# Strassen's seven half-size products for the first feed-forward matrix too, and a batch laid out as values, gate, keys, gate

## The chip, the cores and the metric

The kernel runs on one core of one Trainium2 chip. The metric is device microseconds of one execution. Engines are named as the profile names them: PE (TensorE matmuls), PEld (its weight loads), DVE (VectorE), ACT (ScalarE), POOL (GpSimd) and SP (SyncE, which here issues every DMA). All data are float32; most matrices of the feed-forward part are held as a rounded high part and a low part (`float32r`), and a product of two such matrices takes three matmuls: high by high, high by low, low by high.

## The reference, cut to what matters

```python
s = scale * q @ k^T        # 8 batches, 8 heads, 512 local and 32 global tokens, head size 64
out_l = softmax(s over 32 global keys and a window of +-32) @ v ;  out_g = softmax(all) @ v
x = both, as (batch 8, 576 tokens, 512)
xk = mu_k * x + (1 - mu_k) * x_prev ;  xr = mu_r * x + (1 - mu_r) * x_prev
k = maximum(xk @ w_k, 0.0)                    # w_k: 512 x 1024, "keys"
v = k * k @ w_v                               # w_v: 1024 x 512, "values"
return 1 / (1 + exp(-(xr @ w_r))) * v         # w_r: 512 x 512, the "gate"
```

Weights arrive as float64 words and are decoded on the chip.

## The kernel before, in words

Features lie on the partitions. A batch of 512 local tokens is two halves of 256 tokens (`TOK`), each a `Tokens` object; the 256 global tokens of all batches are one more, done last. For a half, `mix` (L499) makes the high and low parts of xk and xr (DVE, a rounding copy on ACT at L516, the rest on POOL at L517); `squares` (L540) does the keys: per PSUM bank 24 matmuls of 128x256 (`products`, L483 to L485: two blocks of 128 features, four blocks of the sum, three matmuls), then a relu on ACT (L549) and a multiplication on DVE (L551); `gates` (L554) does two banks of 24 and takes tanh on ACT (L564, L566).

The values are Strassen's already, from batch 2 on (`FROM`). With the left matrix cut in 2x2 blocks A and the right one (features by two token halves) in blocks B, seven products replace eight. Sums of blocks of the weights are made once, during batch 1 (`sums_of_values`, L223), and all eight left matrices are kept in DRAM (`scratch`). `load_left` (L253) brings them back in parts of 512 KB, one DMA each, through the five buffers of `leftp`; a product (L632) is 24 matmuls at L639 and uses two parts. `differences` (L614) and `split` (L622) make the right blocks and their high and low parts (ACT L201, then DVE or POOL L202). Three products stand before the keys of a batch's first half (`values_1`), four before those of the second (`values_2`); so a batch goes values, keys, gate, values, keys, gate. Results are multiplied into the gate's tile (`write`, L582) and stored.

Attention for the next batch runs beside the feed-forward part of this one: `together` (L773) deals out steps of the two streams at build time, and a scheduler that plays a timeline then orders each engine's instructions; on the chip each engine runs its list strictly in order. The steps of attention that matter below are the scores (L350), the exponentials (L324: eight in a row on ACT), the scaling (L334 on POOL), transposes (L371, L380, L421) and the weighted sums (L350 again, 117 matmuls in one go). PSUM has eight banks: three ("m") serve the feed-forward part from batch 2 on, four the scores, one the transposes. The last batch and the global tokens have no attention beside them.

Of the kernel before, what the change touches and what calls it, by code (L numbers as in the profile page):

```python
# [55 lines left out]
def local_global_attention_then_rwkv_ffn(  # L56
# [34 lines left out]
    ps2 = ctx.enter_context(tc.tile_pool(name="ps2", bufs=2, space=PSUM))  # L91
# [6 lines left out]
    FIRST_USE = {"m": [ps2] * 2, "s": [ps4] * 4, "t": [ps1, psx], "o": "t"}  # L98
    MIDDLE_USE = {"m": [ps2, ps2, psx], "s": [ps4] * 4, "t": [ps1], "o": "s"}
    LAST_USE = {"m": [ps2, ps2, psx, ps4, ps4, ps4, ps4]}  # L100
# [45 lines left out]
    wk_h = const.tile([P, NC, DF], F32R, name="wk_h")  # L146
    wk_l = const.tile([P, NC, DF], F32R, name="wk_l")

    early_w, early_u = ExitStack(), ExitStack()
    first_chunks = early_w.enter_context(tc.tile_pool(name="first_chunks", bufs=1, reuse_waits="tile"))
# [13 lines left out]
    def load_chunk():  # L166
        n = load_chunk.n
        if n < len(chunks):
            if n < EARLY:
                w64 = first_chunks.tile([P, CH], I64, tag=f"w64_{n}", name="w64")  # L170
            else:
                w64 = stage.tile([P, CH], I64, tag="w64", name="w64")
            nc.sync.dma_start(out=w64, in_=chunks[n][0])
            staged.append(w64)
            load_chunk.n += 1
# [41 lines left out]

    FROM = 2
    LEFT = ("A11", "A21", "A12", "A22", "S2", "S3", "S4", "S1")
    HC = NF // 2  # L220
    scratch = dramp.tile([P, len(LEFT), HC, 2, TOK], F32, name="scratch")

    def sums_of_values():  # L223
        for i in range(HC):
            a = stage.tile([P, 2, 2, TOK], F32, tag="w64", name="a")
            hs, ls = (stage.tile([P, 4, TOK], F32R, tag="w64", name=f"{x}s") for x in "hl")
            for j in range(2):
                f = i + j * HC
                for x, part in enumerate((wv_h, wv_l)):
                    part = part[:, f].bitcast(F32).rearrange("p (e n) -> p e n", e=2)  # L230
                    nc.sync.dma_start(out=scratch[:, 2 * j:2 * j + 2, i, x], in_=part)
                nc.gpsimd.tensor_add(
                    a[:, j], *(w[:, f].bitcast(F32).rearrange("p (e n) -> p e n", e=2) for w in (wv_h, wv_l))
                )
            a11, a21, a12, a22 = (a[:, j, e] for j in range(2) for e in range(2))

            nc.gpsimd.tensor_add(a22, a21, a22)
            nc.gpsimd.tensor_sub(a21, a11, a21)
            nc.gpsimd.tensor_sub(a11, a22, a11)
            nc.gpsimd.tensor_sub(a12, a12, a11)  # L240
            s = a.rearrange("p j e n -> p (j e) n")
            nc.scalar.copy(hs, s)
            nc.vector.tensor_sub(ls, s, hs.bitcast(F32))
            for x, part in enumerate((hs, ls)):
                nc.sync.dma_start(out=scratch[:, 4:8, i, x], in_=part.bitcast(F32))
            yield

    V1 = (("A11", "B11"), ("A12", "B21"), ("S2", "T2"))
    V2 = (("S3", "T3"), ("S1", "T1"), ("A22", "T4"), ("S4", "B22"))
    to_load = [a for a, _ in V1 + V2] * (B - FROM) + ["A11", "A21", "A12", "A22"]  # L250
    left = []

    def load_left():  # L253
        if to_load:
            a = LEFT.index(to_load.pop(0))
            for i in range(0, HC, 2):
                part = leftp.tile([P, 2, 2, TOK], F32R, tag="a", name="a")
                nc.sync.dma_start(out=part.bitcast(F32), in_=scratch[:, a, i:i + 2])
                left.append(part)
# [227 lines left out]
    class Tokens:  # L487
# [5 lines left out]
        def two(self, pool, name, dtype=F32, tag="tmp"):  # L493
            return pool.tile([P, 2, TOK], dtype, tag=tag, name=name)
# [4 lines left out]
        def mix(self):  # L499

            got = []
            for mu, nm in ((mu_k_sb, "k"), (mu_r_sb, "r")):
                got.append((mu, self.wide(f"x{nm}h", F32R), self.wide(f"x{nm}l", F32R)))
            for c0 in range(0, NC, 2):
# [4 lines left out]
                for mu, hi, lo in got:  # L509
                    xf = self.two(tmpp, "xfull")  # L510
                    for j in range(2):
# [3 lines left out]
                        )  # L515
                    nc.scalar.copy(hi[:, both], xf)  # L516
# [3 lines left out]
        def keys_and_gate(self):  # L520
            self.kk_h, self.kk_l = [], []
            for f0 in range(0, NF, 2):
# [7 lines left out]
                nc.gpsimd.tensor_mul(k2, rk, rk)  # L530
# [23 lines left out]
        def gates(self, pool=None):  # L554

            pool = pool or gatep
            self.gate = pool.tile([P, NC, TOK], F32, tag="gate", name="gate")
            for e0 in range(0, NC, 2):
# [4 lines left out]
                with tc.high_priority(None if pool is not gatep else 0):  # L563
# [24 lines left out]

    class Keys:


        def __init__(self, tokens):
            self.tokens = tokens
            self.k, self.parts = {}, {}

# [5 lines left out]
        def block(self, name):  # L601
            if name in ("B12", "B22"):
                tag = {"B12": "kkh0", "B22": "kkh2"}[name]
                self.k[name] = [self.tokens[0].two(mlp, name, tag=tag) for _ in range(2)]
# [5 lines left out]
        def keys(self, t):  # L610
# [11 lines left out]
        def split(self, *names):  # L622
            for b in names:
                self.parts[b] = []
                for val in self.k[b]:
                    tags = Keys.PARTS[Keys.n_parts % len(Keys.PARTS)]
                    Keys.n_parts += 1
                    h, l = (self.tokens[0].two(mlp, f"b{x}", F32R, tag) for x, tag in zip("hl", tags))
# [3 lines left out]
        def product(self, out, b, fresh=True):  # L632
            right = self.parts.pop(b)
            for i in range(HC):
                a, (b_h, b_l) = left[i // 2], right[i // 2]
                for j in range(2):
                    a_h, a_l = (a[:, i % 2, x, j * P:(j + 1) * P] for x in range(2))
# [382 lines left out]
```

## Time and profile before

| | |
|---|---|
| three timed executions | 700.31, 703.33, 703.79 us; median 703.33 us |
| the profiled execution | 702.47 us, of which the span of instructions is 700.6 us |
| mean granted TensorE clock | 0.978 |
| DMA | 123.37 MB, mean 176 GB/s over the span |

Rows of the profile: a group of instructions gives line, engine, operation, what it writes and reads, shape and count, then its busy time in us and the mean length of one in ns, then the idle time of the engine just ahead of it and what ended it. A matmul's length runs from its start to its modelled end; several overlap. Windows give each engine's busy time and number of instructions in a stretch, the granted clock, and the share and rate of the DMA engines. In a timeline the first two numbers are start and length in us.

### The profile page before, as it was taken

What the parts mean: (1) busy time and instruction counts of PE and PEld (TensorE: products, weight loads), DVE (VectorE), ACT (ScalarE), POOL (GpSimd) and SP (SyncE); (2) the same over time, 40 slices, a digit from 0 to 9 for tenths busy, and PEclk for the clock granted to TensorE, in tenths of its full rate; (3) what the DMA queues carried; (4) which work ended last, traced back from release to release, by engine and by line L of the source; (5) the groups of instructions that cost most, each with busy time, mean ns of one, the idle gap of its engine ahead of it and who ended that gap; (6) DMA issues with size and microseconds to landing.
All of it is one profiled execution on the core that took longest, in us unless ns stands there. A gap on an engine that the chain in (4) does not pass through costs nothing.

```text
span 700.6 us, 18622 instructions
## 1 busy us (share of the span) xinstructions
PE 667.4 (95%) x7472; PEld 629.2 (90%) x7472; DVE 417.7 (60%) x1217; ACT 387.9 (55%) x1058; POOL 357.2 (51%) x363
## 2 busy tenths in 40 slices
PE   4879989988999999999999999999999999999997
PEld 2658778978999999999999999999999999999996
DVE  5767977635635375645684557645674656477531
ACT  5756876447445456656557473757465643442530
POOL 5656597864524334573428353645348332642800
PEclk9659999999999999999999999999999999999999
DMA  8732579462312452362909083635727090534665
GB/s 344 288 99 109 200 215 338 157 237 80 127 71 92 132 216 76 122 242 75 359 20 338 25 312 140 222 140 175 279 89 274 2 352 11 196 121 166 216 189 198
DMA packets 43542, 123.37 MB, mean 176 GB/s; under 512 B 4032, under 2 KB 20928, under 8 KB 43456
## 3 DMA queue, kind: packets, MB, share of 16 engines
q1 hardware_dynamic: 43456, 122.18, 49.0%
q8 instruction: 59, 0.97, 0.6%
q14 instruction: 27, 0.22, 0.1%
HBM read 104.86 MB, written 17.30 MB: 174 GB/s over the span
## 4 chain that ended last, share of the span: by engine, by line
PE 75%; DMA 7%; POOL 6%; ACT 5%; DVE 4%; issue 2%; SPq 0%; POOLq 0%; ACTq 0%; DVEq 0%
PE ps_m L639 16%; PE ps_m L483 14%; PE ps_m L484 13%; PE ps_m L485 13%; PE ps_s L350 9%; DMA a<-scratch 3%; PE ps_t L371 3%; ACT Pt L324 2%; PE ps_s L352 2%; DMA w<-w_r 2%; DMA w<-w_v 1%; POOL Pt L334 1%; PE ps_t L421 1%; PE ps_t L350 1%; PE ps_t L380 1%
## 5 line engine op out<-in xcount | busy, mean ns | idle before, releaser
L483 PE MATMUL ps_m<-xkh,wk_h 128*128 128x256 f32 x544 | 155.4, 286 | 4.1 <-ACT xkh L516 2.8
L484 PE MATMUL ps_m<-xkl,wk_h 128*128 128x256 f32 x544 | 154.0, 283 | 0.4 <-POOL xkl L517 0.4
L485 PE MATMUL ps_m<-xkh,wk_l 128*128 128x256 f32 x544 | 153.8, 283 | 0.0
L639 PE MATMUL ps_m<-bh,a 128*128 128x256 f32 x736 | 139.5, 283 | 1.3 <-DMA a<-scratch 1.2
L324 ACT ACTIVATE Pt<-Pt,m 128x160 f32<-128x160 f32 x256 | 106.6, 419 | 26.7 <-DVE m L318 25.0
L639 PEld LDWEIGHTS ps_m<-bh,a 128*128 128x128 f32 x736 | 115.4, 188 | 4.0 <-issue 2.0
L483 PEld LDWEIGHTS ps_m<-xkh,wk_h 128*128 128x128 f32 x544 | 103.8, 191 | 6.1 <-ACT xkh L516 3.4
L334 POOL TENSOR_TENSOR Pt<-Pt,ssum 128x512 f32<-128x512 f32 x64 | 68.6, 1072 | 79.7 <-ACT xrh L516 23.2
L484 PEld LDWEIGHTS ps_m<-xkl,wk_h 128*128 128x128 f32 x544 | 103.9, 191 | 1.3 <-POOL xkl L517 0.7
L485 PEld LDWEIGHTS ps_m<-xkh,wk_l 128*128 128x128 f32 x544 | 103.7, 191 | 0.5 <-issue 0.2
L639 PE MATMUL ps_m<-bl,a 128*128 128x256 f32 x368 | 103.0, 280 | 0.0
L517 POOL TENSOR_TENSOR xkl<-xfull,xkh 128x512 fp32r<-128x512 f32 x34 | 46.9, 1379 | 99.3 <-ACT xkh L516 94.3
L483 PE MATMUL ps_m<-xrh,wr_h 128*128 128x256 f32 x272 | 78.4, 288 | 2.5 <-ACT relu L528 2.5
L551 DVE TENSOR_TENSOR B<-ps_m,relu 128x512 f32<-128x512 f32 x52 | 35.8, 689 | 74.6 <-ACT relu L549 74.5
L484 PE MATMUL ps_m<-xrl,wr_h 128*128 128x256 f32 x272 | 77.4, 285 | 0.0
L485 PE MATMUL ps_m<-xrh,wr_l 128*128 128x256 f32 x272 | 77.3, 284 | 0.0
L549 ACT ACTIVATE relu<-ps_m 128x512 f32<-128x512 f32 x52 | 31.0, 597 | 82.6 <-PE ps_m L485 82.6
L639 PEld LDWEIGHTS ps_m<-bl,a 128*128 128x128 f32 x368 | 69.2, 188 | 0.0
L318 DVE CUSTOM_DVE_ANT_0 Pt<-ps_s,masks 128x160 f32<-128x160 f32 x256 | 65.7, 317 | 2.6 <-PE ps_s L350 2.4
L586 POOL TENSOR_TENSOR gate<-sum,gate 128x512 f32<-128x512 f32 x18 | 26.7, 1481 | 59.3 <-DVE sum L685 38.4
L201 ACT CAST bh<-B 128x512 fp32r<-128x512 f32 x76 | 46.0, 620 | 18.2 <-PE ps_m L639 12.1
L483 PEld LDWEIGHTS ps_m<-xrh,wr_h 128*128 128x128 f32 x272 | 52.2, 192 | 3.2 <-ACT relu L528 2.6
(138 smaller groups left out, 1573.6 us busy)
## 6 DMA issues: line engine op xcount, KB each, us to landing
a<-scratch SPq DMA_DIRECT2D x92, 512.0 KB, 6.2
raw_qk<-qk SPq DMA_DIRECT2D x32, 768.0 KB, 5.5
raw_v<-v SPq DMA_DIRECT2D x32, 640.0 KB, 5.9
out_l<-gate SPq DMA_DIRECT2D x32, 256.0 KB, 4.6
w<-w_k SPq DMA_DIRECT2D x8, 512.0 KB, 9.7
w<-w_v SPq DMA_DIRECT2D x8, 512.0 KB, 4.5
w<-w_r SPq DMA_DIRECT2D x4, 512.0 KB, 4.0
scratch<-wv_h SPq DMA_DIRECT2D x8, 256.0 KB, 3.2
```

Source lines behind the costliest of these rows:

```text
L201: nc.scalar.copy(hi, val)
L318: read = nc.vector.tensor_tensor_reduce(out=Pt[:, i], in0=place(e, t, h), in1=masks[:, e, slots[t][1]], op0=ALU.add, op1=ALU.min, scale=-s ...
L324: nc.scalar.activation(Pt[:, i], Pt[:, i], AF.Exp, bias=low_x[:, i:i + 1], scale=-1.0, accum_out=ssum[:, i:i + 1],)
L334: nc.gpsimd.tensor_mul(out, Pt[:, each, at:at + n], rinv.unsqueeze(2).to_broadcast([P, 4, n]))
L350: self.last = nc.tensor.matmul(*a, **kw)
L483: nc.tensor.matmul(out, w_h[:, i, cols], x_h(i), start=(i == 0), stop=False)
L484: nc.tensor.matmul(out, w_h[:, i, cols], x_l(i), start=False, stop=False)
L485: nc.tensor.matmul(out, w_l[:, i, cols], x_h(i), start=False, stop=(i == n - 1))
L517: nc.gpsimd.tensor_sub(lo[:, both], xf, hi[:, both].bitcast(F32))
L549: nc.scalar.activation(rk, kp, AF.Relu)
L551: nc.vector.tensor_mul(k2[f0 // HC][f0 % HC // 2], kp, rk)
L639: nc.tensor.matmul(out[:, j], w, x[:, i % 2], start=fresh and (i, j, n) == (0, 0, 0), stop=(i, n) == (HC - 1, 2), skip_group_check=True,)
```

## The change

**Keys by Strassen.** From batch 3 on, xk is no longer split half by half: `Keys.mix` (two calls) leaves the four unsplit blocks of xk, and `mixed` makes four differences on DVE and seven high and low pairs (ACT copy, POOL subtraction). `keys` runs `seven` twice, once for each half of the output features. A product of the keys is 12 matmuls and uses one part of the left matrix. So seven products of 12, twice, stand where two halves of 96 matmuls stood. Running sums leave the banks by three copies on ACT and three additions on DVE; of the four outputs three take relu and square in one DVE instruction from SBUF, and the last takes relu on ACT and a product on DVE, from PSUM.

**Sums of the keys' weights** (`sums_of_keys`) are made during batch 2 as those of the values are, but the first additions are on DVE; they go to a second DRAM tensor. After batch 2 the 32 KB per partition of w_k (both parts) are given up for the new blocks. Batch 2 itself, batches 0 and 1 and the gate keep `products`.

**Order.** A batch from 3 on is: all seven products of the values of the batch before, the gate of the first half, the keys of both halves, the gate of the second half. The third gate buffer (`gate3`) is gone: gates alternate between two. `leftp` has six buffers, and six more, in tiles that attention no longer needs, join for the last batch. The global tokens' keys read their left matrix from DRAM as well, ahead of the last batch's values. Sums of the values in batch 1 begin later (`n > FF_STEPS and n % 2`) and wait for a square on POOL (`behind`). The first four weight chunks are staged in tiles of the mix and gate pools, not in a pool of their own, and w_r has its own place from the start.

```diff
+    def sums(home, tag, parts, out, first, after):
+        a = home.tile([P, 2, 2, TOK], F32, tag=tag, name="a")
...
+                behind(after, nc.sync.dma_start(out=out(2 * j, 2 * j + 2, x), in_=parts(x, j)))
+            add = first.tensor_add(a[:, j], parts(0, j), parts(1, j))
+            behind(after, add)
...
+    for b in range(FROM, B - 1):
+        plan(of_values, [a for a, _ in SEVEN])
+        plan(of_keys, [a for a, _ in SEVEN], True)
+    plan(of_keys, FOUR, True)
+    plan(of_values, [a for a, _ in SEVEN])
+    plan(of_values, ("A11", "A21", "A12", "A22"))
...
+    def product(out, right, fresh=True):
+        for i, (b_h, b_l) in enumerate(right):
+            a, home = left.pop(0)
+            for c in range(2):
+                for j in range(2):
+                    a_h, a_l = (a[:, c, x, j * P:(j + 1) * P] for x in range(2))
+                    for n, (w, x) in enumerate(((a_h, b_h), (a_h, b_l), (a_l, b_h))):
+                        nc.tensor.matmul(
...
+            load_left(home)
+            yield
+    def seven(right, done):
+        X, Y, Z = new_bank(), new_bank(), new_bank()
...
+        yield from product(X, right("B11"))
+        copy(c11, X)
+        yield from product(Y, right("B21"))
+        add(Y, c11, 0, 0)
+        yield from product(X, right("T2"), fresh=False)
+        copy(u2, X)
+        yield from product(Z, right("T1"))
+        copy(w, Z)
+        yield from product(X, right("T3"), fresh=False)
+        add(X, w, 1, 1)
+        yield from product(Z, right("B22"), fresh=False)
+        add(Z, u2, 0, 1)
+        yield from product(X, right("T4"), fresh=False)
+        done(1, 0, X)
...
+        def mixed(self):
+            B11, B21, B12, B22 = (self.xv[f"B{i}{j}"] for j in (1, 2) for i in (1, 2))
+            self.x_split("B11", B11)
+            self.x_split("B21", B21)
+            nc.vector.tensor_sub(B11, B12, B11)
...
+        def keys(self):
...
+                    else:
+                        nc.vector.scalar_tensor_tensor(blocks[i, j][n], v, 0.0, v, op0=ALU.max, op1=ALU.mult)
+                yield from seven(lambda b: [self.x[b]], done)
...
+        this.mix(0)
+        for n, _ in enumerate(before.values()):
+            yield
+            if n == 4:
+                this.mix(1)
+            if n == 8:
+                this.mixed()
+        yield from this.tokens[0].gates()
...
+        yield from this.keys()
+        this.split("B11", "B21")
+        this.differences()
+        this.split("T2")
+        yield from this.tokens[1].gates()
```

What the scheduler makes of it, at three places. First PE in the keys of a middle batch. Before, where one bank of keys gives way to the next (`ps_m_5037` to `ps_m_5075`), a bank is filled by one run of 24 matmuls, of which these are the last and the first:

```order
L484 MATMUL ps_m_5037<-xkl_4711,wk_h_167 128x256
L485 MATMUL ps_m_5037<-xkh_4710,wk_l_168 128x256
L483 MATMUL ps_m_5075<-xkh_4710,wk_h_167 128x256
L484 MATMUL ps_m_5075<-xkl_4711,wk_h_167 128x256
L485 MATMUL ps_m_5075<-xkh_4710,wk_l_168 128x256
```

Now, in the keys of a middle batch, the end of product T3 into the bank X (`ps_m_5055`), four matmuls of the gate (`xrh`, `xrl`), and the start of product B22 into the bank Z (`ps_m_5057`); `a_5050` is the part of the left matrix that was loaded:

```order
L649 MATMUL ps_m_5055<-xT3h_4569,a_5027 128x256
L530 MATMUL ps_m_5363<-xrh_4447,wr_h_173 128x256
L531 MATMUL ps_m_5363<-xrl_4448,wr_h_173 128x256
L532 MATMUL ps_m_5363<-xrh_4447,wr_l_174 128x256
L530 MATMUL ps_m_5363<-xrh_4447,wr_h_173 128x256
L649 MATMUL ps_m_5057<-xB22h_4555,a_5050 128x256
L649 MATMUL ps_m_5057<-xB22l_4556,a_5050 128x256
```

The keys change banks every 12 matmuls, and pieces of the second half's gate have moved between them.

Second ACT, about the tanh of a half's gate in a middle batch. Before:

```order
L564 ACTIVATE gate_5183<-ps_m_5284 128x512
L566 ACTIVATE gate_5183<-gate_5183 128x1024
L406 ACTIVATE Pg_5149,ssumg_5151<-Pg_5149,mg_5150 128x576
L475 COPY xT_4781<-ps_s_5210 128x2x2x64
L475 COPY xT_4782<-ps_s_5210 128x2x2x64
```

Now, for the first half of a batch (`gate_4802`), between two copies of sums of the keys (L674), with the attention's copies (`xT`, `PT`) behind it:

```order
L674 COPY c11_4878<-ps_m_4875 128x512
L616 ACTIVATE gate_4802<-ps_m_4803 128x512
L616 ACTIVATE gate_4802<-ps_m_4829 128x512
L618 ACTIVATE gate_4802<-gate_4802 128x1024
L522 COPY xT_4239<-ps_s_4726 128x2x2x64
L522 COPY xT_4240<-ps_s_4726 128x2x2x64
L522 COPY xT_4239<-ps_s_4727 128x2x2x64
L522 COPY xT_4240<-ps_s_4727 128x2x2x64
L420 COPY PT_4862<-ps_t_4863 128x512
L674 COPY u2_4879<-ps_m_4875 128x512
```

The tanh has moved from among the batch's own attention into the keys; `gate_4802` takes the buffer of the first half's gate of the batch before, whose last quarter the seventh product of the values fills.

Third SP, at the end of the values of a middle batch. Before, with attention's loads (`raw_qk`, `raw_v`) in a block of their own:

```order
L710 DMA out_l<-gate_4519 128x2x256
L258 DMA a_6089<-scratch_175 128x1024
L258 DMA a_6531<-scratch_175 128x1024
L710 DMA out_l<-gate_5183 128x2x256
L269 DMA raw_qk_6464<-qk 128x1536
L269 DMA raw_qk_6466<-qk 128x1536
L274 DMA raw_v_6431<-v 128x1280
L274 DMA raw_v_6433<-v 128x1280
```

Now:

```order
L305 DMA a_5807<-scratch_k_184 128x1024
L316 DMA raw_qk_6035<-qk 128x1536
L316 DMA raw_qk_6037<-qk 128x1536
L305 DMA a_5887<-scratch_k_184 128x1024
L822 DMA out_l<-gate_5362 128x2x256
L305 DMA a_5901<-scratch_k_184 128x1024
L822 DMA out_l<-gate_4802 128x2x256
L822 DMA out_l<-gate_5362 128x2x256
L321 DMA raw_v_5973<-v 128x1280
L321 DMA raw_v_5975<-v 128x1280
L305 DMA a_6070<-scratch_k_184 128x1024
```

Loads of the keys' parts now stand between attention's loads and the stores, where there were none.

More of the change, by code (lines that the diff above doesn't have):

```diff
@@ L235, in sums_of_values @@
[L235 to L245, printed above, removed]
```

354 lines of the change are left out of this document (205 added, 149 removed).

## The prediction

> **What bounds the kernel now.** I read the page's first part, then the windows, then what PE waits for.
>
> ```profile
> span 700.6 us, 18622 instructions
> PE 667.4 (95%) x7472; PEld 629.2 (90%) x7472; DVE 417.7 (60%) x1217; ACT 387.9 (55%) x1058; POOL 357.2 (51%) x363
> ```
>
> The windows of 50 us (busy time of PE, PEld, DVE, ACT, POOL, then clock, DMA share, GB/s) say where the missing 5% lie:
>
> ```profile
> 100.00:150.00 50.00, 45.72 (x540) 42.04 (x540) 32.04 (x91) 27.33 (x80) 39.12 (x40) 1.00 0.69 232
> 150.00:200.00 50.00, 46.04 (x559) 43.29 (x563) 25.72 (x84) 25.30 (x70) 23.52 (x27) 0.97 0.40 144
> 200.00:250.00 50.00, 50.00 (x592) 47.45 (x581) 24.20 (x97) 26.87 (x83) 18.66 (x21) 1.00 0.35 123
> ...
> 600.00:650.00 50.00, 50.00 (x434) 50.00 (x433) 32.26 (x48) 19.95 (x35) 22.87 (x18) 1.00 0.46 157
> ```
>
> From 200 us on PE has no gap worth a digit, and the other engines are busy 40 to 60% of the time: a matmul less is its pace less, as long as no new wait appears. In the waits of PE even the values' products, which hang on loads, lose next to nothing (us in total, times, longest):
>
> ```profile
> PE ps_m L639 <- DMA a<-scratch: 1.2, 3, 0.5
> ```
>
> A matmul's price is its pace, not its mean length. In the timeline, two keys with 57 matmuls from one start to the other, and two gates with 45:
>
> ```profile
> 604.28 0.28 PE L483 MATMUL ps_m<-xkh,wk_h 128*128 128x256 f32 x1
> ...
> 610.74 0.28 PE L483 MATMUL ps_m<-xkh,wk_h 128*128 128x256 f32 x1
> ...
> 642.00 0.28 PE L483 MATMUL ps_m<-xrh,wr_h 128*128 128x256 f32 x1
> ...
> 647.40 0.28 PE L483 MATMUL ps_m<-xrh,wr_h 128*128 128x256 f32 x1
> ```
>
> And 48 matmuls of the values, one piece of the chain of waits:
>
> ```profile
> 620.06 5.61 PE ps_m L639 x48
> ```
>
> So a matmul costs 0.113, 0.120 and 0.117 us by these, and not the 0.28 us that its row shows as its length.
>
> **1. Fewer matmuls: -14.0 us.** Keys of a half are 96 matmuls; the group below counts a third of 17 halves (16 local, one global):
>
> ```profile
> L483 PE MATMUL ps_m<-xkh,wk_h 128*128 128x256 f32 x544 | 155.4, 286 | 4.1 <-ACT xkh L516 2.8 <-ACT relu L528 0.7 <-ACT gate L564 0.6
> ```
>
> Five batches go from 10 x 96 = 960 to 5 x 2 x 7 x 12 = 840 matmuls; everything else on PE keeps its count. 120 x 0.117 = 14.0 us (13.6 to 14.4 by the other paces). All of it lies after 200 us, on the path. The Trainium skill ("TensorE: Matmul & The Clock Gate", on back-to-back gaps) gives N / 2.4 + 2.5 ns when warm, 109 ns here; by it the term would be 13.1 us and the time 696 us. The trace's paces are a little longer, and they are used.
>
> **2. Sums of the values later: -1.5 us.** Two of PE's gaps in the stretch where POOL decodes weights and makes the sums, from the timeline:
>
> ```profile
> 119.58 0.38 PE L485 MATMUL ps_m<-kkh,wv_l 128*128 128x256 f32 x1 [1.41 <-POOL wv_l L202]
> ...
> 160.25 0.51 PE L483 MATMUL ps_m<-xkh,wk_h 128*128 128x256 f32 x2 [1.99 <-ACT xkh L516]
> ```
>
> The windows show 4.3 + 4.0 = 8.2 us of PE gaps between 100 and 200 us, where POOL was busy 39 of 50 us with decoding and the sums. The same sums now fall on a POOL that was busy 23.5 of 50. At best the 8.2 us go, at worst a like amount returns later (half of it, as PE has more work in hand there): -8 to +4. I take -1.5, near nothing, since the work only moves.
>
> **3. Sums of the keys: 0.** The values' sums show the prices, a block's addition on POOL and the low part of four on DVE:
>
> ```profile
> L237 POOL TENSOR_TENSOR a<-a 128x256 f32<-128x256 f32 x4 | 3.1, 778 | 0.2
> L243 DVE TENSOR_TENSOR ls<-a,hs 128x1024 fp32r<-128x1024 f32 x4 | 5.2, 1312 | 11.9 <-ACT hs L242 11.9
> ```
>
> In batch 2 POOL gets 16 such additions (12 us), DVE eight first additions of 0.69 us (as L660 below) and four low parts, 11 us, in windows where they were busy 19 and 24 of 50 us. The cover is that slack; without it the loss is bounded by the gaps that the first sums stood beside, 4 us.
>
> **4. Short handovers: +2 us.** A keys' product lasts 12 x 0.117 = 1.40 us, and the next one into the same bank waits for a copy or an addition that may start only when the last matmul ends. From the timeline, the last matmul into a bank of the values, and its copy:
>
> ```profile
> 603.38 0.28 PE L639 MATMUL ps_m<-bh,a 128*128 128x256 f32 x1
> ...
> 603.69 0.59 ACT L664 COPY sum<-ps_m 128x512 f32<-128x512 f32 x1 [0.49 <-PE ps_m L639]
> ```
>
> And the addition, in the groups:
>
> ```profile
> L660 DVE TENSOR_TENSOR sum<-ps_m,sum 128x512 f32<-128x512 f32 x6 | 4.1, 685 | 5.1 <-ACT bh L201 5.1
> ```
>
> From the last start to the copy's end is 0.90 us (an addition: 1.0), so 0.5 us are to spare if ACT is free; the values' products have 24 matmuls, 2.8 us, for the same. There are 4 such handovers in a seven, 40 in all. ACT is busy half the time with pieces of about 0.6 us: one piece ahead costs 0.1 us, 4 us in all. Gate matmuls and attention lie between most of them in PE's order, so half: 2. Bounds 0 and, with two pieces ahead each time, 0.7 x 40 = 28.
>
> **5. The gate waits for a store: +2.5 us.** Without `gate3` the tanh of a batch's first half writes the tile whose last quarter the seventh product of the values before fills and SP stores. The product into the gate on DVE (least, median and longest in ns):
>
> ```profile
> L586 DVE TENSOR_TENSOR gate<-ps_m,gate x8: 677/692/692, 342.7 to 696.7; 128x512 f32<-128x512 f32 x8
> ```
>
> The store's issue and its landing:
>
> ```profile
> L710 SPq DMA_DIRECT2D out_l<-gate x32: 377/388/395, 128.5 to 686.3; - x32
> ...
> DMA to landing us min/median/max: 2.1/4.6/6.9
> ```
>
> The tanh:
>
> ```profile
> L564 ACT ACTIVATE gate<-ps_m 128x512 f32<-128x512 f32 x34 | 20.1, 592 | 11.3 <-PE ps_m L485 11.3
> ```
>
> And, from the chain, the weighted sums of two pairs of heads that lie one batch apart:
>
> ```profile
> 519.33 4.02 PE ps_s L350 x117
> ...
> 592.09 4.01 PE ps_s L350 x117
> ```
>
> 0.69 + 0.39 + 4.6 + 0.59 = 6.3 us (3.8 to 8.6). Queued behind the tanh on ACT are the attention's copies and the keys' copies; the second product of the keys waits for the tanh's bank. PE's order has some 45 matmuls and 64 of the weighted sums' 117 to do meanwhile: 5.3 + 2.2 = 7.5 us. At the median nothing is lost, at the longest landing 1.1 us. With more loads about, I take 0.5 us in each of five batches. Bounds 0 and 17 (rival B).
>
> **6. Loads: +2 us.** 14 more parts per batch and 8 for the global tokens, 78 of 512 KB:
>
> ```profile
> a<-scratch SPq DMA_DIRECT2D x92, 512.0 KB, 6.2
> raw_qk<-qk SPq DMA_DIRECT2D x32, 768.0 KB, 5.5
> raw_v<-v SPq DMA_DIRECT2D x32, 640.0 KB, 5.9
> ```
>
> And a window in which the DMA engines were full:
>
> ```profile
> 330.00:340.00 10.00, 10.00 (x146) 9.45 (x143) 4.78 (x11) 5.88 (x13) 7.25 (x7) 1.00 0.95 348
> ```
>
> A batch lasts 72.8 us (519.33 to 592.09 above) and would move 28 parts, 4 + 4 loads of attention and 1 MB of output, 21.5 MB, which at the 348 GB/s of the window above is 62 us: 85% of the time. Behind the last heads PE has some 850 matmuls, 99 us, and 58 parts with 2.6 MB of output to move, 33 MB, 95 us: close to even, with twelve buffers of slack. The waits before were 1.2 us in six passes of the values; I take 2 for eleven passes of values and keys. Bounds 0 and 14 (rival C).
>
> **7. POOL in the values' pass: +1 us.** In a middle batch POOL's order, from the first split of xk's blocks to the last split for the values, has 19 operations of 128x512 and the scaling of one set of scores (3 us). Two in a row in the timeline:
>
> ```profile
> 379.14 2.54 POOL L202 TENSOR_TENSOR bl<-B,bh 128x512 fp32r<-128x512 f32 x2
> ```
>
> And the spread of one (least, median, longest):
>
> ```profile
> L202 POOL TENSOR_TENSOR bl<-B,bh x36: 1274/1302/1624, 297.3 to 664.0; 128x512 fp32r<-128x512 f32 x36
> ```
>
> 19 x 1.27 + 3 = 27 us, while PE has 190 matmuls and some 6.5 us of attention, 28.7 us: even. A gain is excluded, since nothing on PE gets shorter by it; above, at 1.62 us each, it is 5 us a batch in the four batches with attention beside the pass, 20 in all. I take 1 for the lot, by the median, which is nearest.
>
> The sum: -14.0 - 1.5 + 2 + 2.5 + 2 + 1 = -8.0 us. The profiled execution took 702.47 us, its span and 1.9 us about it; 694.5 us by it. The median of the three runs, 703.33, stands 0.9 above, so 695 us.
>
> **The rivals.** A measurement of this kernel tells about 0.5%, 3.5 us, from no change: faster is below 699.8, slower above 706.8.
>
> A, waits eat the gain. Term 4 at 0.2 us on each of 40 handovers, 8 us, and term 7 at 1 us a batch: -14 - 1.5 + 8 + 2.5 + 2 + 4 = +1, 704 us on the median's scale. For it: ACT's slack of 0.5 us; against: before, PE never waited on the values' copies. 0.15.
>
> B, slower: the store stands behind attention's loads. If the 1.57 MB of two `raw_qk` (4.5 us at 348 GB/s) are in flight ahead of it, the tanh ends at 10.8 us against a cover of 7.5: 3.3 us, 16.5 in five batches, in place of 2.5: 709 us. It turns the result slower from 2.9 us a batch on. For it: SP's order has these loads four and five places ahead; against: the median landing before, 4.6 us, held loads ahead of it too. 0.09.
>
> C, the DMA rate. A part at 348 GB/s takes 1.51 us and lasts 1.40 in a product. If buffers don't bridge that, 0.11 x 14 us per pass over eleven passes, 17 us, come in place of 2: 710. Against: gates and attention consume nothing meanwhile. The Trainium skill ("DMA: Bandwidth & Descriptors", its table of limits) puts a core's HBM limit at about 358 GB/s, which would speak for this rival in the stretch without attention. The 348 agrees. 0.06.
>
> D, POOL is shut out. DVE gains ten operations with two SBUF inputs per batch, about 0.69 us each; if each holds up POOL in the values' pass for its length, four to six fall there and term 7 becomes 3 us in four batches, 12 in place of 1: 706. The Trainium skill ("SBUF — State Buffer", on the shared port pair) says that such a DVE operation and a GpSimd one exclude each other for the whole instruction; POOL's 1.27 to 1.62 us for one shape agree. 0.05.
>
> E, more is won early: term 2 at -8 and waits of 4 us in all: -18, 685 us. For it: the gaps there are real; against: the sums have to go somewhere. 0.09.
>
> **How the numbers follow.** My forecast, 688 to 699, 0.56; E 0.09; A 0.15, D 0.05, B 0.09, C 0.06. Faster: 0.65 with nearly all of E, 0.66 with an edge of A. Same: the rest of A and most of D, 0.18. Slower: B, C and a little of D, 0.16. The range of 8 in 10 takes in A and D and cuts the lower half of E and the upper parts of B and C: 684 to 707.
>
> **What would show it.** In the changed profile: L649 has 2040 matmuls of keys and values; PE stays at 50 of 50 us from 200 us on in most windows; waits of PE on L674 copies in total under 4 us (4), of PE behind the tanh, L616, under 1 us a batch (5), on `a` under 3 us (6), on POOL's L203 under 2 us (7); gaps of PE between 100 and 200 us of 5 to 9 us (2). I am wrong if PE shows a gap of over 2 us in every batch, ACT standing at L616 for a DMA being the first place to look, or if L649's pace is off 0.117 by more than 0.003.

## The result, and the profile after

The changed kernel takes 750.88 us (median of four runs, 749.21 to 751.98); the kernel before, on the same chip, 702.96. The ratio is 1.0687, 95% interval 1.0652 to 1.0722: slower by 48 us, where 8 us less were forecast. The profiled execution has a span of 747.1 us, 46.5 more than before. The page's first part:

```profile
span 747.1 us, 18721 instructions
...
PE 669.7 (90%) x7352; PEld 627.2 (84%) x7352; DVE 508.0 (68%) x1269; ACT 397.6 (53%) x1077; POOL 415.5 (56%) x398
```

PE has its 120 matmuls fewer, but 77 us of gaps instead of 33. DVE has 52 instructions more and is busy 90 us longer: 1.7 us for each new one, while an operation of 128x512 took 0.69. The windows (PE, PEld, DVE, ACT, POOL, clock, DMA share, GB/s):

```profile
100.00:150.00 50.00, 50.00 (x612) 47.73 (x612) 26.07 (x90) 25.76 (x79) 20.53 (x21) 1.00 0.33 114
150.00:200.00 50.00, 49.12 (x591) 46.23 (x588) 30.58 (x95) 26.78 (x80) 33.55 (x34) 1.00 0.58 203
200.00:250.00 50.00, 44.07 (x483) 42.13 (x483) 26.68 (x73) 25.77 (x74) 35.70 (x37) 0.97 0.71 244
250.00:300.00 50.00, 46.15 (x511) 42.47 (x509) 44.40 (x102) 28.46 (x78) 29.04 (x28) 0.97 0.63 206
```

The 8.2 us of gaps between 100 and 200 us are down to 0.9, but between 200 and 300 us stand 9.8. Before there were none; the second half of that stretch in the kernel before:

```profile
250.00:300.00 50.00, 50.00 (x634) 47.19 (x633) 30.52 (x101) 30.62 (x90) 24.89 (x24) 1.00 0.33 123
```

What PE waits for in the changed kernel (total, times, longest):

```profile
PE ps_t L427 <- DVE PT L420: 24.3, 5, 7.3
...
PE ps_m L649 <- ACT u L674: 7.1, 1, 7.1
...
PE ps_m L649 <- DMA a<-scratch_k: 1.5, 1, 1.5
...
PE ps_m L530 <- ACT gate L616: 0.3, 1, 0.3
```

The first line is new: three times, a batch apart, PE's next transposes wait 6.3 to 7.3 us (and once 3.8) for DVE to copy the last ones (`PT`, L420) out of the only bank for them. In the kernel before, PE waited for that copy once:

```profile
PE ps_t L421 <- DVE PT L373: 1.3, 1, 1.3
```

What DVE does meanwhile in the changed kernel, in one values' pass (start and length in us):

```profile
386.50 1.67 DVE L767 TENSOR_TENSOR B<-B,T 128x512 f32<-128x512 f32 x1
388.09 1.84 DVE L559 TENSOR_TENSOR diff<-xT 128x256 f32<-128x256 f32 x2
389.86 0.47 DVE L563 SCALAR_TENSOR_TENSOR xB<-diff,mu_k_sb,xT 128x256 f32<-128x256 f32 x1
390.26 0.47 DVE L563 SCALAR_TENSOR_TENSOR xfull<-diff,mu_r_sb,xT 128x256 f32<-128x256 f32 x1
...
392.12 1.49 DVE L563 SCALAR_TENSOR_TENSOR xB<-diff,mu_k_sb,xT 128x256 f32<-128x256 f32 x1
393.53 1.50 DVE L563 SCALAR_TENSOR_TENSOR xfull<-diff,mu_r_sb,xT 128x256 f32<-128x256 f32 x1
394.96 1.53 DVE L563 SCALAR_TENSOR_TENSOR xB<-diff,mu_k_sb,xT 128x256 f32<-128x256 f32 x1
396.41 0.47 DVE L563 SCALAR_TENSOR_TENSOR xfull<-diff,mu_r_sb,xT 128x256 f32<-128x256 f32 x1
...
402.74 0.68 DVE L420 COPY PT<-ps_t 128x512 f32<-128x512 f32 x1
```

And POOL in the same stretch:

```profile
386.07 1.55 POOL L203 TENSOR_TENSOR xB11l<-xB,xB11h 128x512 fp32r<-128x512 f32 x1 [5.79 <-ACT xB11h L202]
387.58 1.74 POOL L570 TENSOR_TENSOR xrl<-xfull,xrh 128x512 fp32r<-128x512 f32 x1
391.85 1.47 POOL L203 TENSOR_TENSOR xB21l<-xB,xB21h 128x512 fp32r<-128x512 f32 x1 [2.54 <-ACT xB21h L202]
393.28 1.47 POOL L570 TENSOR_TENSOR xrl<-xfull,xrh 128x512 fp32r<-128x512 f32 x1
394.81 1.39 POOL L203 TENSOR_TENSOR bl<-T,bh 128x512 fp32r<-128x512 f32 x1
```

Lay the two lists side by side. The multiplications at 389.86 and 390.26, while POOL is idle, take 0.47 us; the same multiplications at 392.12, 393.53 and 394.96, each with a subtraction of POOL beside it, take 1.5: each ends 0.3 us after POOL's operation has ended. The two engines take turns. DVE is recorded as busy without a pause, but much of that time it waits for its turn; the copy that PE needs stands behind all these operations in its list.

### The profile page after: what moved, and what is told of

Its sections match the earlier page's. It is cut to its first block, busy times and chain, and to the rows that moved or that the text cites. A ratio compares the mean times of both kernels' runs of the same rounds, so it can differ in the third digit from the quotient of the medians.

```text
span 747.1 us, 18721 instructions
## 1 busy us (share of the span) xinstructions
PE 669.7 (90%) x7352; PEld 627.2 (84%) x7352; DVE 508.0 (68%) x1269; ACT 397.6 (53%) x1077; POOL 415.5 (56%) x398
## 4 chain that ended last, share of the span: by engine, by line
PE 50%; DVE 28%; ACT 8%; POOL 7%; issue 4%; DMA 2%; SPq 0%; DVEq 0%; POOLq 0%; ACTq 0%
PE ps_m L649 23%; DVE xfull L563 5%; PE ps_m L530 5%; PE ps_m L531 5%; PE ps_s L397 5%; PE ps_m L532 5%; ACT Pt L371 5%; DVE diff L559 4%; DVE xB L563 4%; PE ps_t L418 2%; DVE B L767 2%; PE ps_t L393 2%; DVE Pt L365 1%; DVE PT L420 1%; POOL a L242 1%
## 5 line engine op out<-in xcount | busy, mean ns | idle before, releaser
L649 PE MATMUL ps_m<-bh,a 128*128 128x256 f32 x736 | 144.3, 292 | 8.7 <-ACT u L674 7.1
L649 PEld LDWEIGHTS ps_m<-bh,a 128*128 128x128 f32 x736 | 120.7, 198 | 10.0 <-ACT u L674 7.3
L649 PE MATMUL ps_m<-bl,a 128*128 128x256 f32 x368 | 106.3, 289 | 0.0
L649 PEld LDWEIGHTS ps_m<-bl,a 128*128 128x128 f32 x368 | 72.9, 198 | 0.6 <-POOL gate L638 0.6
L530 PE MATMUL ps_m<-xkh,wk_h 128*128 128x256 f32 x192 | 57.1, 300 | 2.3 <-ACT xkh L569 2.0
L531 PE MATMUL ps_m<-xkl,wk_h 128*128 128x256 f32 x192 | 56.8, 296 | 1.0 <-POOL xkl L570 1.0
L570 POOL TENSOR_TENSOR xrl<-xfull,xrh 128x512 fp32r<-128x512 f32 x34 | 48.5, 1426 | 15.7 <-ACT xrh L569 15.7
L532 PE MATMUL ps_m<-xkh,wk_l 128*128 128x256 f32 x192 | 55.9, 292 | 0.0
L203 POOL TENSOR_TENSOR bl<-B,bh 128x512 fp32r<-128x512 f32 x36 | 51.0, 1426 | 7.5 <-ACT bh L202 7.5
L531 PEld LDWEIGHTS ps_m<-xrl,wr_h 128*128 128x128 f32 x272 | 52.4, 192 | 0.6 <-issue 0.2
L532 PEld LDWEIGHTS ps_m<-xrh,wr_l 128*128 128x128 f32 x272 | 52.3, 192 | 0.6 <-issue 0.6
L563 DVE SCALAR_TENSOR_TENSOR xfull<-diff,mu_r_sb,xT 128x256 f32<-128x256 f32 x64 | 48.7, 774 | 5.5 <-POOL xkl L570 5.5
L559 DVE TENSOR_TENSOR diff<-xT 128x256 f32<-128x256 f32 x64 | 44.1, 724 | 9.4 <-ACT xT L522 9.3
L371 ACT ACTIVATION_READ_ACCUMULATOR Pt<-Pt,m 128x1 f32 x256 | 48.4, 189 | 0.0
```

The costliest lines, as they stand in the source:

```text
L203: engine.tensor_sub(lo, val, hi.bitcast(F32))
L371: nc.scalar.activation(Pt[:, i], Pt[:, i], AF.Exp, bias=low_x[:, i:i + 1], scale=-1.0, accum_out=ssum[:, i:i + 1],)
L530: nc.tensor.matmul(out, w_h[:, i, cols], x_h(i), start=(i == 0), stop=False)
L531: nc.tensor.matmul(out, w_h[:, i, cols], x_l(i), start=False, stop=False)
L532: nc.tensor.matmul(out, w_l[:, i, cols], x_h(i), start=False, stop=(i == n - 1))
L559: nc.vector.tensor_sub(self.shape(diff[:, j]), self.cur(c0 + j), self.prev(c0 + j))
```

## Experiments

The ratio is to the kernel before, whose median lay between 702.4 and 703.6 us in each set; a difference of about 1 us between runs of two sets therefore says nothing. e2, g2 and k1 leave out work that the result needs; they are there to price it.

| run | what | us | ratio, 95% interval |
|---|---|---|---|
| e1 | second PT copy on ACT | 751.4 | 1.0673, 1.063 to 1.0717 |
| e2 | low parts of the keys' blocks left out | 736.3 | 1.0458, 1.0408 to 1.0508 |
| e3 | low parts on DVE | 714.4 | 1.0152, 1.0106 to 1.0198 |
| e4 | keys by whole products, rest kept | 726.2 | 1.0319, 1.0278 to 1.0361 |
| g1 | e3, and the sums' additions on DVE | 708.6 | 1.0078, 1.0052 to 1.0103 |
| g2 | e3, and the arithmetic of the sums left out | 698.4 | 0.9938, 0.9913 to 0.9963 |
| g3 | e3, and the values' sums early | 704.7 | 1.0018, 0.9997 to 1.0039 |
| g4 | g1, and all other low parts of xk and xr on DVE | 722.1 | 1.0253, 1.0197 to 1.031 |
| h1 | e3, g1 and g3 together | 719.4 | 1.0207, 1.017 to 1.0245 |
| h2 | h1, and the keys' sums in batch 1 | 711.2 | 1.0105, 1.0073 to 1.0138 |
| h3 | kernel before, low parts on DVE | 704.6 | 1.0024, 0.9999 to 1.005 |
| i1 | changed kernel, values' sums early | 742.3 | 1.0569, 1.0543 to 1.0595 |
| i2 | g3, keys' sums in batch 1 | 710.5 | 1.01, 1.0077 to 1.0123 |
| i3 | g3, xr's low parts back on POOL | 724.1 | 1.0297, 1.0273 to 1.032 |
| j1 | g3, products with the gate on DVE | 701.9 | 0.9985, 0.9971 to 0.9998 |
| j2 | g3, keys' sums spread | 704.4 | 1.0019, 0.9999 to 1.0039 |
| j3 | j1 and j2 together | 701.0 | 0.9972, 0.9957 to 0.9986 |
| k1 | j3, arithmetic of the sums left out | 700.1 | 0.9954, 0.9937 to 0.9971 |

**Is it this copy, DVE's list, or POOL beside it?** Four runs ask this. e1:

```diff
-        copy = nc.vector.tensor_copy if e else nc.scalar.copy
+        copy = nc.vector.tensor_copy if e and r.slots[0][0].b < 4 else nc.scalar.copy
```

> The second copy of a pair's transposed weights (PT, L420) is on ACT instead of DVE, for attention of batches 4 to 7. Theory T (DVE is late as a whole: its operations with two SBUF inputs and POOL's exclude each other, and whatever stands behind them in DVE's order waits): PE's 24 us of waits on that copy go, but DVE is as late as it was, so the additions of the running sums and the scores' minima behind it hold PE instead: 733 to 745 us. Rival P (only the place of this one copy is wrong): the 24 us go and about 6 us of cold clock with them: 718 to 724 us. Rival H (the cause is the short handovers of the keys' products, not DVE): no change, 748 to 752 us.

751.4 us: rival P is out. The number is the one that rival H gave, but its reason is not there. The waits on the copy went, and others that hang on DVE's list took their place: the running sum's addition (L669) first, then an ACT copy (`PTg`) that stands behind exponentials waiting for DVE's minima:

```profile
PE ps_m L530 <- DVE c L669: 12.6, 3, 5.4
PE ps_t L418 <- ACT PTg L428: 9.2, 4, 4.0
PE ps_m L649 <- ACT u L674: 7.0, 1, 7.0
```

So theory T's mechanism held, and its 6 to 18 us of gain did not come: DVE was as late for the next operation that PE needs. e2, with the seven low parts of the keys' right blocks left out:

```diff
...
-            split(val, h, l, nc.gpsimd)
...
+            nc.scalar.copy(h, val)
+            self.x[name] = h, h
```

> The seven low parts of the keys' right blocks are left out in batches 3 to 7 (the high part is multiplied in their place, so PE has the same matmuls): 35 subtractions less on POOL, DVE's list as it was. Theory T: DVE's multiplications into xB (885 ns on average) fall to 500 to 650 ns, PE's waits on the PT copy from 24 us to under 8, and the time to 715 to 732 us. Rival Q (DVE's list is too long in the values' pass by its own work, whatever POOL does): the lengths and the waits stay, 745 to 752 us.

736.3 us, 14.6 less. DVE has the same 1269 instructions and is busy 480.8 us instead of 508.0: rival Q is out. T's sizes were too large (PE's waits on the copy are 8.7 us, not under 8, and the time is 4 us above T's range), since twelve other subtractions of POOL stay in the pass. DVE's 40 multiplications into xB (busy us, mean ns), first in the changed kernel:

```profile
L563 DVE SCALAR_TENSOR_TENSOR xB<-diff,mu_k_sb,xT 128x256 f32<-128x256 f32 x40 | 35.2, 885 | 0.0
```

and with the 35 subtractions left out:

```profile
L563 DVE SCALAR_TENSOR_TENSOR xB<-diff,mu_k_sb,xT 128x256 f32<-128x256 f32 x40 | 27.8, 711 | 0.0
```

e3 gives the work to DVE instead (three such lines: these blocks, xr, and the values' right blocks):

```diff
-            split(val, h, l, nc.gpsimd)
+            split(val, h, l, nc.vector)
```

> All low parts that POOL subtracts in the values' pass of batches 3 to 7 (those of the keys' right blocks, of xr and of the values' right blocks) are subtracted on DVE, some 17 a batch. Theory T: on POOL each takes 1.3 to 1.5 us and keeps DVE's two-input operations out for as long; on DVE it takes 0.6 to 0.7 us, so the work that the two do one after the other gets shorter by 10 us a batch: 710 to 735 us, DVE's L563 at 0.48 us. Rival Q: DVE gets 11 us more in a stretch where it is late already, the waits of PE grow by 5 to 11 us a batch: 775 to 800 us.

714.4 us, 36.5 less, with more work on the engine that was late. Theory T holds, rival Q is wrong by 60 us and more. The page's first part:

```profile
PE 671.7 (95%) x7352; PEld 623.4 (88%) x7352; DVE 509.0 (72%) x1372; ACT 395.4 (56%) x1077; POOL 286.1 (40%) x295
```

and the same multiplications in the groups:

```profile
L563 DVE SCALAR_TENSOR_TENSOR xB<-diff,mu_k_sb,xT 128x256 f32<-128x256 f32 x40 | 19.7, 503 | 0.0
```

DVE does 103 instructions more in 1.0 us more; POOL has 129 us less to do. e4 undoes the Strassen keys alone: batches 3 to 7 go through the code of batch 2, and the sums and the new buffers stay with batch 2.

```diff
-        if b == FROM:
+        if b >= FROM:
...
```

> Keys of batches 3 to 7 by whole products again, with the rest of the change kept (values first, gate, second keys, gate; tanh from PSUM on two gate buffers; the sums of the keys made in batch 2, the global keys from DRAM; seven values' products before the first keys). 120 matmuls more on PE, 14 us. Theory T and any that blames the work about the keys' right blocks: the 7-us waits go, 700 to 715 us. Rival O (the batch's order, the gate or the sums in batches 1 and 2 make the loss): 745 to 765 us.

726.2 us lies between the two expectations. Without the work about the keys' blocks the kernel is 24.6 us faster, though PE has 14 us more to do; but 23 us of loss stay with as many matmuls as before the change, so there is a second cause. PE's gaps between 200 and 300 us, 9.8 in the changed kernel, are still 8.8 in e4. About 12 of the 23 us are lost early: the weighted sums that begin at 295.3 us in the kernel before begin at 307.4 in e4. The rest lies in the later batches, and no run tells which part of the new order makes it.

One more suspect is in the traces. In the changed kernel ACT stands at the tanh, L616, for the store of the gate's tile, once in each of the five batches:

```profile
ACT gate L616 <- DMA out_l<-gate: 26.9, 5, 7.8
```

In e3 that wait is 0.5 us, so it could be what e3 took away. It is not: in g3, which is faster still (704.7 us), ACT stands there nearly as long.

```profile
ACT gate L616 <- DMA out_l<-gate: 23.5, 5, 6.6
```

PE itself waits 0.3 us for the tanh in the changed kernel and 0.6 in g3.

**The second cause.** In e3 PE still lost 10 us of gaps between 184 and 346 us. Two tests on top of e3: g2 stores blocks of the weights in place of their sums, without the arithmetic, and g3 lets the values' sums begin with batch 1 again:

```diff
-                if n > FF_STEPS and n % 2:
-                    next(sums, None)
+                next(sums, None)
```

> On top of the low parts on DVE (714.4 us): the arithmetic of the weights' sums is left out (blocks are stored in the sums' places, so that all stores and loads stay). Theory S: the 10 us of PE's gaps between 184 and 346 us and the cold clock behind them go, 697 to 704 us. Rival D (the stores' traffic, 16 MB in two batches, or the batches' new order makes the loss): 711 to 716 us.

> On top of the low parts on DVE (714.4 us): the sums of the values begin with batch 1, as before the change, and not in its second half. Theory S (the sums cost PE wherever they lie; later, in a stretch with attention's scores and the keys' sums close behind, they cost more than earlier): the early gaps of 6 us come back, the two gaps at 216 and 234 us (4.6 us and the cold clock) go: 709 to 715 us. The forecast's term 2 (moving them gains): 716 to 722 us.

g2 takes 698.4 us, 16.1 less than e3: the arithmetic is the cost, and rival D is out. g3 takes 704.7 us, 9.7 less, which puts 9.7 of the 16 on the values' sums in their later place. This is better than either expectation: the early gaps did not come back. With the sums where they were before the change, PE has 0.3 us of gaps between 100 and 200 us in g3 and 0.6 in i1, against 8.2 in the kernel before. So it was not the move of the sums that closed those gaps; which other part of the change did is not shown. i1 makes the same edit on the changed kernel itself.

> The changed kernel with the values' sums from the start of batch 1, and nothing else (the low parts stay on POOL). Theory T+S (two causes in different stretches, which add: 36 us by DVE and POOL taking turns in the values' passes, 10 us by the later sums): 750.9 less 10, 738 to 744 us. Rival (the low parts' move made the earlier sums pay, alone they do not): 747 to 753 us.

742.3 us, 8.6 less, within the range expected: the two causes add. Undone together, e3's 36.5 us and the 16.1 of g2 account for 52.6 of the 56 us by which the forecast was missed.

**A control.** h3 moves the same low parts from POOL to DVE in the kernel before.

> A control: the kernel before the change, with the low parts of xk, xr and the values' right blocks from batch 2 on moved from POOL to DVE. Theory T (the move pays only where DVE's queue holds PE; before, PE had no waits after 200 us): no gain, 700 to 707 us, although DVE's two-input operations get shorter. Rival (the moves help by themselves, and the changed kernel should be set against a kernel before that has them too): 690 to 698 us.

704.6 us, no gain. DVE's operations got shorter there too; the 64 multiplications for xr went from 648 ns on average in the kernel before to 534 (first the kernel before, then h3):

```profile
L512 DVE SCALAR_TENSOR_TENSOR xfull<-diff,mu_r_sb,xT 128x256 f32<-128x256 f32 x64 | 39.7, 648 | 7.9 <-POOL xkl L517 5.0 <-POOL xrl L517 2.5
L512 DVE SCALAR_TENSOR_TENSOR xfull<-diff,mu_r_sb,xT 128x256 f32<-128x256 f32 x64 | 32.4, 534 | 3.3 <-POOL xkl L517 3.1
```

but PE hardly waits for DVE in either: 4.8 us in all in the kernel before and 4.5 here, against 40 in the changed kernel. Taking turns cost time only where the queue behind it held PE.

**From the other side.** i3 puts only xr's 20 low parts back on POOL, in g3.

> Low parts on DVE and the values' sums early (704.7 us), but xr's low parts, 20 of them, back on POOL. Theory T (each shuts DVE out for 1.3 us in the values' pass, where DVE's queue holds the PT copy): slower, 709 to 722 us. Rival L (DVE is the fuller engine by now and gains from having 0.68 us less for each): 698 to 703 us.

724.1 us: 19.4 us for 20 subtractions, somewhat over T's range. DVE has 20 instructions fewer than in g3 and is busy 6.5 us longer (514.5 against 508.0). The multiplications into xB are longer again:

```profile
L563 DVE SCALAR_TENSOR_TENSOR xB<-diff,mu_k_sb,xT 128x256 f32<-128x256 f32 x40 | 26.0, 662 | 0.0
```

**More of the same cure.** g1 moves the sums' additions to DVE, g4 the other low parts too, h1 joins e3, g1 and g3, and h2 and i2 move the keys' sums into batch 1.

> On top of the low parts on DVE (714.4 us): all additions of the weights' sums, of values and of keys, on DVE instead of POOL. Theory S (between 184 and 346 us the sums make DVE and POOL take turns and hold PE, some 18 us of the 25 that are still missing): an addition of 128x256 takes 0.8 us on POOL and shuts DVE out, on DVE about 0.45 us, so eight blocks get shorter by 1.5 to 2.7 us each: 702 to 711 us. Rival L (DVE's own load is what is late there): DVE gets 24 us more, 718 to 730 us.

> As the kernel with all sums on DVE, and also the low parts of xk and xr of batches 0 to 2 and of the global tokens on DVE: POOL keeps the scaling, the decoding and the products with the gate. Theory T/S: 28 subtractions of 1.3 to 1.5 us leave POOL and cost DVE 0.68 us each: 697 to 708 us. Rival L: 718 us or more.

> Three moves together on the changed kernel: the low parts in the values' pass on DVE, the sums' additions on DVE, and the values' sums from the start of batch 1. Alone on top of the first, the second gave 6 us and the third 10 us. Theory S (each takes away waits in another stretch, 243 to 280 us and 184 to 235 us): 696 to 701 us, at or below before. Rival L (DVE full, the two gains are the same slack): 703 to 709 us.

> As the kernel with the three moves, and the sums of the keys in the second half of batch 1 instead of in batch 2 (they need only w_k, which is there since batch 0). Theory S (batch 2 has the full DVE between 260 and 295 us): 691 to 699 us, with no gap of PE left between 240 and 300 us. Rival: the sums cost the same wherever they lie, 698 to 706 us.

> Low parts on DVE, the sums of the values from the start of batch 1 (704.7 us with these two), and the sums of the keys in the second half of batch 1 instead of batch 2, their additions on POOL as they were. Theory S (the place decides: batch 2's DVE is full, batch 1's is not): 696 to 703 us. Rival (the sums cost the same wherever they lie): 704 to 710 us.

g1 gains 5.8 us (708.6), within theory S's range. The other four miss S's ranges: g4 is 13.5 us slower than g1, h1 (719.4) is slower than each of its parts, and the keys' sums in batch 1 end at 711.2 (8.3 below h1, which h2 is built on) and 710.5 (5.8 above g3, which i2 is built on).

g4's time is the one that rival L, DVE's own load, gave, but the traces do not bear its reason out. g4's extra subtractions lie in batches 0 to 2 and in the global tokens. From the weighted sums at 306.0 us to those at 590.0 lie batches whose code is the same as in g1, without one of the subtractions that were moved. g4 takes 284.0 us for them; g1, from 303.0 to 572.6, takes 269.6. What differs there is the order: each edit makes the scheduler order every engine anew. h1 takes 269.6 us for that stretch, just as g1 does. What it loses to g1 it loses before, and whether DVE's load or the order does that is not shown. So a few microseconds of one edit, up or down, say little about its cause here.

**Towards a faster version.** What POOL still did in the values' pass of g3 were 18 products with the gate's tile, 1.5 to 2.9 us each on average, where DVE then took 0.68 to 0.78 (in j3). Twelve of them:

```profile
L638 POOL TENSOR_TENSOR gate<-c,gate 128x512 f32<-128x512 f32 x6 | 17.2, 2870 | 119.1 <-DVE c L669 119.1
L638 POOL TENSOR_TENSOR gate<-w,gate 128x512 f32<-128x512 f32 x6 | 9.2, 1539 | 18.1 <-DVE w L669 18.1
```

```diff
-            (nc.vector if v.tensor.name.startswith("ps_") else nc.gpsimd).tensor_mul(o, v, o)
+            nc.vector.tensor_mul(o, v, o)
```

> Low parts on DVE, the values' sums early (704.7 us), and the 18 products with the gate's tile that POOL still makes in the values' passes on DVE too. Theory T: each takes 1.4 to 2.4 us on POOL and shuts DVE out, 0.68 us on DVE: 699 to 704 us. Rival L: no gain, 704 to 710 us.

> Low parts on DVE, the values' sums early, and the four blocks of the keys' sums spread over the keys of both halves of batch 2 instead of the first half alone. Theory S (they cost because they stand close together, 243 to 280 us): 698 to 703 us, under 2 us of PE's gaps between 255 and 280 us instead of 5. Rival: the gaps move with them, 704 to 709 us.

> Both of these together. If both pay: 693 to 700 us, below the kernel before. If the scheduler's new order takes it back, as it did with the sums on DVE: 705 to 715 us.

> The fastest version so far (701.0 us) with the arithmetic of the weights' sums left out; stores and loads stay. By landmarks that version still spends 151.4 us between the 5th and the 9th weighted sums, where the kernel before spends 142.3. Theory S (those 9 us are the sums): 690 to 694 us. Rival (it is the batch's order and the stores): 698 to 702 us.

j1 takes 701.9 us, 2.8 less than g3; j2 takes 704.4, no gain. j3 takes 701.0, which is 50 us below the changed kernel and 0.28% below the kernel before (0.14 to 0.43%), short of the 693 to 700 hoped for. k1 leaves the sums' arithmetic out of j3 and gains 0.9 us only, no more than sets differ by: theory S is wrong for this version, in which the sums cost next to nothing. j3 has 120 matmuls fewer than the kernel before and is 2.2 us faster, not 14. Its page:

```profile
PE 664.0 (95%) x7352; PEld 621.8 (89%) x7352; DVE 511.7 (73%) x1390; ACT 397.3 (57%) x1077; POOL 245.7 (35%) x277
```

PE is busy 3.4 us less than before the change (667.4), where 14 were expected. So most of what is missing lies inside PE's busy time, where a length of 0.28 us at a pace of 0.117 can cover a wait of 0.16. It is missing in the batches with Strassen's keys and attention side by side: from the weighted sums at 296.3 us to those at 594.7 j3 takes 298.4 us, where the kernel before, from 295.3 to 591.8, takes 296.4, though PE has about 70 matmuls fewer there. PE's visible gaps in that stretch are 5.9 us, before 0.6. Which edit these waits belong to stays open.

## Why the prediction was wrong, step by step

**What bounds the kernel** failed first. From "busy 40 to 60% of the time" it followed that a matmul less is its pace less. The mean hid the order. This change puts both halves' mixing, the differences, the splits of seven blocks and the splits for the values into one pass of 28 us, and DVE is full there: in the pass shown above it is busy from 390 to 405 us without a pause.

**Term 7 (+1) is the step that failed most: 36.5 us by e3, which includes whatever the scheduler's new order did.** It counted POOL's 27 us against PE's 28.7 and asked whether POOL's results come late. They did not: PE waited 2.7 us for L203. DVE's time in the pass was not counted at all, nor what stands behind it. Rival D had the rule, but let DVE hold up POOL, at 0.69 us each. The trace shows both held up, and DVE more: about 1.0 us for each of its multiplications, while POOL's subtractions above take 1.4 to 1.7 us instead of 1.3. The Trainium skill ("SBUF — State Buffer", section "SBUF: two separate sides", on the shared port pair) says that a DVE operation with two SBUF inputs and a GpSimd one that reads SBUF exclude each other: whichever starts first blocks the other for the whole instruction. The trace agrees: 0.47 us alone, 1.5 beside POOL. With that reading an estimate from the rows at hand was possible: 19 operations of 1.3 us take up to 25 us of DVE's time, in a pass of 28. The gaps that came of it were 6.3 to 7.3 us a batch. The kernel before had the sign already, in the 648 ns of its multiplications for xr against 0.47 us alone.

**Terms 2 and 3 (-1.5 and 0): together 16.1 us on top of e3.** The early gaps went nearly whole, from 8.2 us to 0.9, but not through the move of the sums, as g3 and i1 show. The forecast took that work to be neutral in its new place, since "POOL was busy 23.5 of 50". It cost 8.6 us alone and 9.7 on e3. The rest of g2's gain, about 6 us, is by subtraction what the keys' sums and the values' sums in their early place still cost; they were taken as hidden in slack, and that slack was again a mean over 50 us.

**Term 1 (-14.0)** had the right count, 2040 matmuls at L649, and the right pace. 48 of them in the changed kernel, from the chain:

```profile
712.72 5.54 PE ps_m L649 x48
```

0.115 us each against 0.117. But no run's median is more than 4.1 us below the kernel before, so the 14 us themselves were never seen as time.

**Terms 4, 5 and 6** were about right as far as they show. Term 5 had its mechanism: ACT did stand at the tanh for the store in every batch, up to 7.8 us, and PE had enough to do meanwhile; it lost 0.3 us by it (in e3 3.1; forecast 2.5). Loads cost 1.5 us (in g3 4.1; forecast 2). Of the handovers one wait of 7.1 us shows, in the last batch; there ACT's copy stands behind a cast that waits for DVE, and e3, which shortens DVE's list, has it no more. Rivals B and C, a store and the DMA rate, decided nothing, and C's ceiling was too low: the changed kernel moved 382 GB/s from 672 to 691 us, where 348 was taken as full. D was the nearest, with the wrong victim and 706 us.

Of the signs named, "a gap of over 2 us in every batch" came: 3.8, 6.3, 6.3, 7.3 and 7.1 us in batches 3 to 7. The waits at L674 (7.1 us), on L203 (2.7) and the early gaps (0.9) fell outside their bounds too; the tanh and the loads stayed within. ACT at L616 was the wrong first place to look, although ACT did stand there; DVE at L420 was the right one.

## What to carry to other kernels

Before work is moved into a stretch, add up each in-order engine's list in that stretch, with POOL's and DVE's two-input operations in one sum, and look at who stands at the end of it; a mean over a batch says nothing. Moving work from the idler of the two (POOL) to the busier (DVE) took 36 us off here, because a subtraction of 1.3 us that shut DVE out became one of 0.69; the same move without a waiter gained nothing. An engine's wait is no loss by itself either: ACT stood 27 us for a store, and PE lost 0.3. Where a kernel has two causes of loss, undo them one by one and together: here one pair added (i1) and another did not (h1). And where a scheduler orders everything anew after each edit, look in the trace for the stretch in which the time changed: g4's 14 us lay in batches that the edit does not touch.

## What the runs showed of the hardware

Not every DVE operation takes turns with POOL. A running sum's addition has one input in PSUM and one in SBUF; all 48 of them in the changed kernel took 0.64 to 0.69 us. One of them:

```profile
404.90 0.68 DVE L669 TENSOR_TENSOR c<-ps_m,c 128x512 f32<-128x512 f32 x1
```

ran while POOL had a subtraction from 404.39 to 406.13 us:

```profile
404.39 1.74 POOL L203 TENSOR_TENSOR bl<-B,bh 128x512 fp32r<-128x512 f32 x1
```

A gap of PE can cost more than itself. Around the gap of 6.3 us at 397 us (busy time of PE, then the others, then the granted clock):

```profile
395.00:399.00 4.00, 2.16 (x40) 1.73 (x39) 4.00 (x6) 2.09 (x4) 2.59 (x3) 1.00 0.81 236
399.00:403.00 4.00, 0.00 (x0) 0.00 (x0) 4.00 (x6) 0.68 (x3) 2.75 (x2) 0.73 0.15 57
403.00:407.00 4.00, 3.53 (x17) 3.53 (x18) 4.00 (x16) 3.34 (x10) 3.85 (x3) 0.50 0.00 0
```

The clock is at half for the 4 us after it, and matmuls start 0.213 us apart instead of 0.117:

```profile
404.39 0.63 PE L649 MATMUL ps_m<-bh,a 128*128 128x256 f32 x2
404.81 0.41 PE L649 MATMUL ps_m<-bl,a 128*128 128x256 f32 x1
405.03 0.63 PE L649 MATMUL ps_m<-bh,a 128*128 128x256 f32 x2
```

Three matmuls in 0.64 us. By an estimate from these rows, 18 of them fit between 403.8 and 407.6 us, where the pace is back; at 0.096 us too much each that is 1.7 us more for this gap. The Trainium skill ("TensorE: Matmul & The Clock Gate", Part 1) has the clock at half after an idle window of about 3.4 us and the start-to-start time then at N / 1.2 GHz, 0.213 us for 256 columns. The trace agrees in the second. The first is not borne out as a threshold for gaps: h1 has a gap of 2.2 us just before 339.4 us, with shorter ones behind it, and then the clock is down:

```profile
330.00:340.00 10.00, 7.80 (x67) 7.60 (x66) 10.00 (x17) 3.19 (x6) 7.18 (x6) 1.00 0.64 206
340.00:350.00 10.00, 9.41 (x69) 8.35 (x68) 7.19 (x26) 8.16 (x26) 3.49 (x5) 0.83 0.46 152
```

In e3 a gap of 2.4 us before 218.1 us is followed by a clock of 0.50 from 220 to 222 us, while behind one of 2.2 us before 236.2 us it stays at 1.00. So a gap of this length may cost the clock or may not.
